# Forward transforms of two convolutions as three passes over high and low parts, with one transform table and kernel rows in natural order

## The chip, the core and the metric

The kernel runs on one core of a Trainium2 chip. The metric is the device time in microseconds (us) of one execution. The core has five engines that matter here: TensorE (PE, with its weight loads PEld), VectorE (DVE), ScalarE (ACT), GpSimd (POOL) and SyncE (SP). POOL and SP are used for issuing DMA transfers. Each engine runs its own list of instructions, whose order is fixed when the kernel is built; an instruction that waits for another engine holds up those behind it on its list.

## The reference

The reference is one transformer-like block on a sequence of L = 2048 tokens with D = 576 channels. All arrays are float32. A state-space convolution with a long kernel comes first, then a dense network of two layers:

```
P = exp((A * dt)[:, :, None] * pos)          # D x 128 x 2048 modes
K = 2 * einsum("dn,dnl->dl", C, P).real      # one kernel of length 2048 for each channel
y = irfft(rfft(u, 2L) * rfft(K, 2L))[:L] + u * D_skip

h = layernorm(x) * (1 + ca) + sa
x = x + ga * conv(h)
h = layernorm(x) * (1 + cb) + sb
x = x + gb * (relu(h @ w1) @ w2)             # 576 -> 4608 -> 576
```

The six vectors `sa, ca, ga, sb, cb, gb` come from silu(c) @ w_mod.

## The kernel before

The 2048 tokens are cut into four blocks of 512. For each block there is a convolution step, `conv(s)` for s = 0 to 3, and a feed-forward block of 36 steps, each of 128 hidden units. Counting through, steps 0 to 35 are block 0, 36 to 71 block 1, 72 to 107 block 2, and the rest block 3. The first 110 steps are done singly, and the rest, two at a time, in another form.

A single step g has two halves on PE. `first(g)` is 14 passes of 128x512 into the PSUM tile `hps` (L1368, two buffers). ACT turns it into `hh` (L1373, relu, the rounded high part), and DVE into `hl` (L1374, what the rounding left). `second(g)` is 14 passes into five accumulators `acc` (L1394): 9 or 10 of them use `hh`, the others `hl`. PE's order is `first(g)`, `second(g-1)`, `first(g+1)`, and so on. In the steps of block 0 DVE also makes the low parts of the weights (L1338, L1349, L1350), which later blocks load from DRAM.

While feed-forward block b runs, the next convolution, `conv(b+1)`, is produced in small pieces between its passes. `conv` is a Python generator whose `yield` values are estimated microseconds of DVE (or `None` for a piece on PE). The function `step(g)`, called four times in a step, takes pieces as long as the sum of estimates is below rate(b) times the number of calls. That sets when the pieces are written; the scheduler of the Tile framework then fixes the order on each engine.

A convolution of block s uses blocks of the FFT of the signal `U` and of the kernel `K`, in two halves of channels p = 0 and 1. It works like this:

- The kernel rows are loaded into a tile `kt` (one buffer, so the tile of p = 1 can only be loaded when the transforms of p = 0 have read it). `load_kt` does that with one DMA from POOL, L1291.
- `norm1` makes the normalised input `h` on DVE (L937, L938).
- `mm_K` and `mm_U` are the forward transforms: for each p, 8 fp32 matmuls of 128x288, each into one PSUM buffer (L854) that ACT empties into `Z` (L855). They use two tables of cosines and sines, `fcU` for the signal and `fcK` for the kernel. `fcK` has its rows in the order in which the kernel's rows stand in `kt`.
- Butterflies on DVE (L868 to L882) finish the transforms to `U_s_p` and `K_s_p`; L1001 and L1003 combine `K` with the block before it, `R`, which POOL loads from DRAM.
- `product` sums over earlier blocks: groups of DVE operations on 128x1152 (L1034, L1038, L1040). A product that isn't the first goes through a scratch tile `T` of half size, of which there are two buffers.
- The inverse: butterflies to `V_s_p`, 8 matmuls for each p (`ps_i`, L1061), and an addition to x (L1066).
- Statistics, transposes on PE (`ps_t`, L1155), and `xf`, `xh`, `xl`, `xs` (L1159 to L1168): these are what the feed-forward block of s works on.

The tiles of one size share a pool of seven buffers (`spec`), so a new one waits for an old one to be read.

Of the kernel before, what the change touches and what calls it, by code (L numbers as in the profile page):

```python
# [10 lines left out]
F32 = mybir.dt.float32  # L11
# [40 lines left out]
class KGen:  # L52
# [10 lines left out]
    def v(self, out, a, b, op):  # L63
        self.tc.keep_in_program_order(self.nc.vector.tensor_tensor(out, a, b, op=op))  # L64
# [511 lines left out]
class Body:  # L576
# [34 lines left out]
    def early(self, kg):  # L611

        nc, I, sm = self.nc, self.I, self.sm
        x2 = self.x2[0] = self.x2p[0].tile([P, 4, D], F32, tag="x2", bufs=1, name="x2_0")
        nc.sync.dma_start(out=x2, in_=I["x"][0:512, :].rearrange("(m n) d -> m n d", n=4))
        self.fcU, self.fcK, self.gc = (
            sm.tile([P, 4, 2, P], F32, name=n) for n in ("fcU", "fcK", "gc")
        )
        for t, n in ((self.fcK, "fck"), (self.fcU, "fcu"), (self.gc, "gc")):
            nc.sync.dma_start(out=t, in_=I[n])  # L620
        kept = self.tc.keep_in_program_order
        self.mv1 = mv = sm.tile([P, 4, 5], F32, name="mv1")
        for i in range(4):
            yield
            st = sm.tile([P, 2, 6], F32, tag="st", bufs=8, name="st0")
            for p in range(2):
                kept(nc.vector.bn_stats(out=st[:, p], in_=x2[:, i, p * PC : (p + 1) * PC]))
            kept(nc.vector.bn_aggr(out=mv[:, i, 0:2], in_=st))
        yield
        kept(nc.scalar.activation(mv[:, :, 2], mv[:, :, 1], AF.Sqrt, bias=self.eps))  # L630
        yield
        kept(nc.vector.reciprocal(mv[:, :, 3], mv[:, :, 2]))
        kept(nc.vector.scalar_tensor_tensor(
            mv[:, :, 4], mv[:, :, 0], -1.0, mv[:, :, 3], op0=ALU.mult, op1=ALU.mult
        ))
        self.h0 = h = kg.pw.tile([P, 4, D], F32, tag="W2", bufs=5, name="h_0")
        for i in (0, 2, 1, 3):
            kept(nc.scalar.activation(
                h[:, i], x2[:, i], AF.Identity, scale=mv[:, i, 3:4], bias=mv[:, i, 4:5]
            ))  # L640
        yield
        self.kt0 = kg.kt0
        kept(self.skip(self.kt0, 0, nc.vector))
        for i in (0, 2, 1, 3):
            kept(nc.vector.tensor_tensor(h[:, i], h[:, i], self.m["ca"], op=ALU.mult))
            kept(nc.vector.tensor_tensor(h[:, i], h[:, i], self.m["sa"], op=ALU.add))
        self.wm = {}
        for nm in ("sb", "cb"):
            self.wm[nm] = kg.pw.tile([P, 5, D], F32, tag="W2", bufs=5, name=f"wm_{nm}")
        yield  # L650
# [290 lines left out]
    def conv(self, s):  # L941
# [26 lines left out]
            h = self.spec(f"h_{s}").rearrange("p a b c -> p a (b c)")  # L968
        hv = h.rearrange("m n (dd p q) -> m n dd p q", dd=4, p=2)

        def mm_U(p, Z):
            return self.transform(lambda n2: hv[:, n2, :, p], self.fcU, Z, s == 0)

        def mm_K(p, Z):
            ktv = kt[p].rearrange("p (t dd g) q -> p t dd g q", t=2, g=2)
            if s == 0 and p == 1:
                self.skip(kt[p], p, Kept(self.tc, nc.gpsimd))
            src = lambda n2: ktv[:, n2 // 2, :, n2 % 2]
            if s == 0 and p == 1:
                return self.transform1(src, self.fcK, self.fcKn, Z)  # L980
            return self.transform(src, self.fcK, Z, s == 0)

        def spec_U(p, Z):
            U = self.spec(f"U_{s}_{p}")
# [92 lines left out]
        if s == 0:  # L1077
            yield from mm_K(0, ZK)
            yield from mm_U(0, ZU)
            Z1 = self.spec("Z")  # L1080
            yield from mm_U(1, Z1)
            for hook in ("first", "late", "rows"):
                yield hook
            kt[1] = kernel_tile(1)
            yield "weights"
            yield "mod"
            yield "mod"
            yield "mod"
            yield "high"
            yield from spec_U(0, ZU)  # L1090
            yield from spec_U(1, Z1)
            yield from spec_K(0, ZK)
            ZK = self.spec("Z")
            yield from mm_K(1, ZK)
            self.save(self.Rd[0][0], Ks[0], Kept(self.tc, nc.gpsimd))
        else:
            yield from both(self.norm1(x2, h), mm_K(0, ZK))
            kt[1] = kernel_tile(1)
            ZU = self.spec("Z")
            yield from both(spec_K(0, ZK), mm_U(0, ZU))  # L1100
            Z1 = self.spec("Z")
            yield from both(spec_U(0, ZU), mm_U(1, Z1))
            ZK = self.spec("Z")
            first[0] = self.load(self.Ud[0][0], "Ua")
            yield from both(spec_U(1, Z1), mm_K(1, ZK))
# [182 lines left out]

    def load_kt(self, kt, s, p, eng):
        kd = self.kd[s][p]  # L1290
        eng.dma_start(  # L1291
            out=kt,
            in_=bass.AP(tensor=kd.tensor, offset=kd.offset, ap=[[72, P], [9216, 16], [1, 72]]),
        )
# [409 lines left out]
            yield  # L1704

    def rate(self, b):
        return (2.15, 1.8, 1.4, 0.5)[b]


def after(n, g):  # L1710
# [79 lines left out]
```

## Time and profile before

| what | value |
|---|---|
| time, median of 3 runs | 1318.13 us (1313.81 to 1322.35) |
| the profiled execution: its own time | 1324.17 us |
| the profiled execution: span | 1322.4 us |
| mean granted clock of PE | 0.943 |
| PE busy | 1210.1 us, 92% |
| DVE busy | 993.3 us, 75% |
| ACT busy | 518.8 us, 39% |
| POOL busy | 161.1 us, 12% |

The span is the time from the first to the last instruction of the profiled execution. PE counts as busy while a matmul is in its pipeline, so 100% does not mean that passes follow each other at their shortest distance; the distance of two passes is read from the chain of waits or the timeline. In the chain, a row gives the start, the time and the number of instructions of one piece of the work that set the end. In the table of windows a row gives the busy time of each engine in a stretch of the span. Block 0 of the feed-forward network runs until about 553 us, block 1 until about 829, block 2 until about 1094.

### The profile page before, as it was taken

To read this page: it belongs to the slowest core of one execution; us is meant where nothing else is said; L and a number is where in the kernel's file an instruction comes from. 1 tells how busy PE (TensorE), PEld (TensorE's weight loads), DVE (VectorE), ACT (ScalarE), POOL (GpSimd) and SP (SyncE) were. 2 spreads that over 40 slices of the span, in tenths; PEclk is the share of its full clock that TensorE was granted. 3 is DMA by queue.
4 is the path that set the end of the run, shared out by engine and by line. 5 is a ranking of instruction groups with operands and counts; after the bars stand their busy time and mean duration, and the time that the engine had idled before them with its cause. 6 is when DMAs were issued, how large, how long until landed. Compare 5 with 4: busy or idle time off the path is not lost.

```text
span 1322.4 us, 27077 instructions
## 1 busy us (share of the span) xinstructions
PE 1210.1 (92%) x11094; PEld 973.6 (74%) x11094; DVE 993.3 (75%) x1538; ACT 518.8 (39%) x902; POOL 161.1 (12%) x256
## 2 busy tenths in 40 slices
PE   4665586899989998999999999999999999999998
PEld 3454464677767787787677887887888888998997
DVE  7899988999986999689468995467997237555543
ACT  5788423222223422622243225433222365434431
POOL 1676411011000100110001000100000000000000
PEclk9556787999989999999899999999999999999999
DMA  9758972988878967799779995877996658666641
GB/s 273 269 201 307 327 275 79 351 289 321 312 267 294 344 228 274 249 405 343 251 266 340 348 353 155 274 220 263 373 388 191 180 166 256 190 190 190 193 142 63
DMA packets 118032, 343.81 MB, mean 260 GB/s; under 512 B 17772, under 2 KB 21652, under 8 KB 107156
## 3 DMA queue, kind: packets, MB, share of 16 engines
q1 hardware_dynamic: 101332, 226.04, 51.0%
q0 software_dynamic: 16064, 114.67, 22.9%
q8 instruction: 87, 1.43, 0.4%
q10 hardware_dynamic: 512, 1.38, 0.3%
q14 instruction: 37, 0.30, 0.1%
HBM read 260.63 MB, written 81.40 MB: 259 GB/s over the span
## 4 chain that ended last, share of the span: by engine, by line
PE 71%; DVE 16%; DMA 7%; issue 3%; ACT 1%; POOL 1%; SPq 0%; ACTq 0%; DVEq 0%
PE acc L1394 28%; PE hps L1368 21%; PE hps L1495 7%; PE ps_f L854 5%; DMA L1d<-w 4%; PE kps L73 2%; PE kps L521 2%; PE ps_i L1061 2%; PE ph L73 2%; DVE T L486 1%; DVE W1r L488 1%; DMA x<-in_x_dram 1%; DVE Y L1040 1%; DVE T L64 1%; DVE w L1338 1%
## 5 line engine op out<-in xcount | busy, mean ns | idle before, releaser
L1394 PE MATMUL acc<-w,hh 128*128 128x512 f32 x1008 | 323.1, 403 | 3.2 <-ACT hh L1373 2.7
L1368 PE MATMUL hps<-xh,w 128*128 128x512 f32 x880 | 307.4, 410 | 0.7 <-ACT xh L49 0.7
L1394 PEld LDWEIGHTS acc<-w,hh 128*128 128x128 f32 x1008 | 187.4, 188 | 44.0 <-ACT hh L1373 3.6
L1368 PEld LDWEIGHTS hps<-xh,w 128*128 128x128 f32 x880 | 168.6, 192 | 38.7 <-ACT xh L49 1.3
L1394 PE MATMUL acc<-w,hl 128*128 128x512 f32 x504 | 195.1, 401 | 1.5 <-DVE hl L1374 1.5
L1343 ACT ACTIVATE w<-r 128x576 fp32r<-128x576 f32 x141 | 96.6, 685 | 229.7 <-PE acc L1394 195.2
L1368 PE MATMUL hps<-xl,w 128*128 128x512 f32 x440 | 175.7, 400 | 0.0
L1373 ACT ACTIVATE hh<-hps 128x512 fp32r<-128x512 f32 x110 | 65.7, 597 | 242.1 <-PE hps L1368 237.4
L1374 DVE SCALAR_TENSOR_TENSOR hl<-hps,hh 128x512 fp32r<-128x512 f32 x110 | 75.4, 685 | 113.1 <-ACT hh L1373 112.5
L1394 PEld LDWEIGHTS acc<-w,hl 128*128 128x128 f32 x504 | 94.3, 189 | 22.8 <-DVE hl L1374 3.0
L1333 ACT ACTIVATE w<-r 128x640 fp32r<-128x640 f32 x124 | 90.8, 732 | 42.7 <-DMA L1d<-w 42.1
L1368 PEld LDWEIGHTS hps<-xl,w 128*128 128x128 f32 x440 | 84.1, 191 | 18.3 <-DVE xl L49 0.4
L1040 DVE TENSOR_TENSOR Y<-Y,T 128x1152 f32<-128x1152 f32 x60 | 79.3, 1348 | 0.0
L73 PE MATMUL kps<-W,W 128*32 128x16 f32 x2304 | 39.4, 210 | 42.8 <-POOL W L70 28.4
L1368 PE MATMUL hps<-xs,w 128*128 128x512 f32 x220 | 78.0, 421 | 0.0
L855 ACT ACTIVATE Z<-ps_f 128x288 f32<-128x288 f32 x120 | 49.0, 410 | 71.6 <-PE ps_f L854 69.7
L73 PEld LDWEIGHTS kps<-W,W 128*32 128x32 f32 x2304 | 34.7, 142 | 56.4 <-POOL W L70 31.0
L521 PEld LDWEIGHTS kps<-W1r,W2r 128*32 128x32 f32 x3456 | 45.1, 113 | 38.8 <-issue 20.8
L521 PE MATMUL kps<-W1r,W2r 128*32 128x48 f32 (+2 forms) x3456 | 52.4, 202 | 15.9 <-ACT ker L531 9.3
L1503 DVE TENSOR_TENSOR C<-C,hps 128x256 f32<-128x256 f32 x17 | 7.1, 420 | 63.0 <-PE hps L1495 63.0
L1394 PE MATMUL acc<-hh,w 128*128 128x512 f32 x126 | 50.7, 402 | 0.0
L1394 PE MATMUL acc<-hl,w 128*128 128x512 f32 x126 | 49.9, 396 | 0.0
(307 smaller groups left out, 2197.9 us busy)
## 6 DMA issues: line engine op xcount, KB each, us to landing
r<-in_w_dram SPq DMA_DIRECT2D x144, 320.0 KB, 3.9
r<-in_w_dram SPq DMA_DIRECT2D x144, 288.0 KB, 4.9
w<-L2d SPq DMA_DIRECT2D x108, 288.0 KB, 4.1
w<-L1d SPq DMA_DIRECT2D x92, 320.0 KB, 3.9
W2r<-W2d POOLq DMA_DIRECT2D x18, 1536.0 KB, 8.5
W2d<-W SPq DMA_DIRECT2D x12, 1536.0 KB, 8.5
Ua<-Ud POOLq DMA_DIRECT2D x15, 1152.0 KB, 9.5
W<-W1d POOLq DMA_DIRECT2D x18, 768.0 KB, 9.4
```

The source lines that it names most:

```text
L73: self.tc.keep_in_program_order(self.nc.tensor.matmul(*args, **kw))
L521: nc.tensor.matmul(ps[32 * dd : 32 * dd + 32, q, :], W2[:, r, ch], W1[:, r, ch], start=(r == 0), stop=(r == 1),)
L854: nc.tensor.matmul(o, fc[:, n2, c, :], src(n2), start=True, stop=True)
L855: ev = nc.scalar.activation(Z[:, n2, c], ps[:, :PC], AF.Copy)
L1040: v(y, y, T, op=op or ALU.add)
L1333: copy(g - 1)(w1[g][:, 0], r1[g], AF.Copy)
L1343: copy(g)(w[:, 0:D], r2[g], AF.Copy)
L1368: nc.tensor.matmul(ps, a, x, start=(i == 0), stop=(i == 13))
L1373: nc.scalar.activation(hh, ps, AF.Relu)
L1374: nc.vector.scalar_tensor_tensor(hl, ps, 0.0, hh, op0=ALU.max, op1=ALU.subtract)
L1394: nc.tensor.matmul(acc[i], a, x, start=(f == 0 and seen[i] == 1), stop=(f == NF - 1 and seen[i] == (3 if i < 4 else 2)),)
L1495: nc.tensor.matmul(out, l, m, start=(i == 0), stop=(i == len(ops) - 1))
```

## The change

For the convolutions 2 and 3 (`s > 1`, the third and fourth) a forward transform is no longer an fp32 matmul. Its input is split in two parts: ACT rounds it to fp32r (the high part), DVE subtracts that from the input (the low part). `split` does it in two pieces of 128x576 for each call, into the two `half` buffers that the products' `T` also uses. The table is split in the same way, once, by `table`, before convolution 2; the parts go to the places of `fcK` and `fcU`. A transform is then three fp32r passes into the same PSUM tile: high by high, high by low, low by high.

Two further edits belong to it. The kernel rows of the convolutions 1 to 3 are loaded in natural order, so that one table serves `U` and `K`: eight DMAs, each into every eighth partition. The rates at which pieces of convolutions are taken are 1.86 and 1.46 instead of 1.8 and 1.4 in blocks 1 and 2.

```diff
@@ conv(s)
+        def split(x, name):
+            hi, lo = (
+                self.half(name + n).rearrange("p n (a b) -> p n a b", a=4).bitcast(F32R)
+                for n in "hl"
+            )
+            for i in range(2):
+                h, l = (t[:, 2 * i : 2 * i + 2] for t in (hi, lo))
+                nc.scalar.activation(h, x[i], AF.Copy)
+                v(l, x[i], h, op=ALU.subtract)
+                yield 0.8
+            return lambda n2: (hi[:, n2], lo[:, n2])
+
+        def table():
+            f = lambda t: t.rearrange("p n c k -> p (n c k)")
+            sm, shape = self.sm, [P, 4, 2, P]
+            hi = sm.tile(shape, F32R, tag="fcK", bufs=1, name="fch")
+            nc.scalar.activation(f(hi), f(self.fcU), AF.Copy)
+            t = self.spec("fct").rearrange("p a b c -> p (a b c)")[:, :1024]
+            v(t, f(self.fcU), f(hi), op=ALU.subtract)
+            yield 1.5
+            lo = sm.tile(shape, F32R, tag="fcU", bufs=1, name="fcl")
+            nc.scalar.activation(f(lo), t, AF.Copy)
+            self.parts = hi, lo
+
+        def thirds(p, Z, x, name):
+            hi, lo = self.parts
+            src = yield from split(x, name)
+            for n2 in (0, 2, 1, 3):
+                xh, xl = src(n2)
+                for c in range(2):
+                    ps = self.cps.tile([P, 512], F32, tag="cps", bufs=self.nps, name="ps_f")
+                    o = ps[:, :PC].rearrange("p (a b) -> p a b", a=4)
+                    fh, fl = hi[:, n2, c], lo[:, n2, c]
+                    for i, (a, b) in enumerate(((fh, xh), (fh, xl), (fl, xh))):
+                        nc.tensor.matmul(o, a, b, start=(i == 0), stop=(i == 2))
+                    nc.scalar.activation(Z[:, n2, c], ps[:, :PC], AF.Copy)
+                    yield None
+
         def mm_U(p, Z):
+            if s > 1:
+                return thirds(p, Z, [hv[:, 2 * i : 2 * i + 2, :, p] for i in range(2)], "hs")
             return self.transform(lambda n2: hv[:, n2, :, p], self.fcU, Z, s == 0)
...
+            if s > 1:
+                x = kt[p].rearrange("p (t dd g) q -> p t g dd q", t=2, g=2)
+                return thirds(p, Z, [x[:, i] for i in range(2)], "ks")
...
-            return self.transform(src, self.fcK, Z, s == 0)
+            return self.transform(src, self.fcU if s else self.fcK, Z, s == 0)
...
+            if s == 2:
+                yield from table()
@@ load_kt
+        if s:
+            for b in range(8):
+                eng.dma_start(
+                    out=kt[b::8],
+                    in_=bass.AP(
+                        tensor=kd.tensor, offset=kd.offset + 1152 * b,
+                        ap=[[72, 16], [9216, 16], [1, 72]],
+                    ),
+                )
+            return
@@ rate(b)
-        return (2.15, 1.8, 1.4, 0.5)[b]
+        return (2.15, 1.86, 1.46, 0.5)[b]
```

The line numbers of the changed kernel are later ones: `hl` is L1429, `acc` L1449, `hps` L1423, the products L1077, L1081 and L1083, the inverse L1104, the transposes L1200, the weights' low parts L1393, L1404 and L1405.

The change also moves work that it doesn't name. The first place is DVE in block 0, from the `hl` of step 21 on. Before, the normalisation of convolution 1 (`h_1`) and its first butterfly follow at once:

```order
L1374 SCALAR_TENSOR_TENSOR hl_5448<-hps_5429,hh_5447 128x512
L1338 TENSOR_TENSOR w1_5382<-r1_5269,w1_5382 128x640
L937 SCALAR_TENSOR_TENSOR h_1_5225<-x2_1_5203,mv_5309,m_ca_469 128x576
L937 SCALAR_TENSOR_TENSOR h_1_5225<-x2_1_5203,mv_5312,m_ca_469 128x576
L938 SCALAR_TENSOR_TENSOR h_1_5225<-h_1_5225,mv_5309,m_sa_551 128x576
L938 SCALAR_TENSOR_TENSOR h_1_5225<-h_1_5225,mv_5312,m_sa_551 128x576
L937 SCALAR_TENSOR_TENSOR h_1_5225<-x2_1_5203,mv_5315,m_ca_469 128x576
L937 SCALAR_TENSOR_TENSOR h_1_5225<-x2_1_5203,mv_5318,m_ca_469 128x576
L938 SCALAR_TENSOR_TENSOR h_1_5225<-h_1_5225,mv_5315,m_sa_551 128x576
L938 SCALAR_TENSOR_TENSOR h_1_5225<-h_1_5225,mv_5318,m_sa_551 128x576
L868 TENSOR_TENSOR W_5389<-Z_5226 128x576
L869 TENSOR_TENSOR W_5389<-Z_5226 128x576
```

In the changed kernel the same place, again from the `hl` of step 21 on, has only the weights' low parts (`w1`, `w2`) between one `hl` and the next:

```order
L1429 SCALAR_TENSOR_TENSOR hl_5462<-hps_5443,hh_5461 128x512
L1393 TENSOR_TENSOR w1_5389<-r1_5276,w1_5389 128x640
L1404 TENSOR_TENSOR w2_5543<-r2_5358,w2_5543 128x64
L1405 TENSOR_TENSOR w2_5543<-r2_5358,w2_5543 128x512
L1393 TENSOR_TENSOR w1_5471<-r1_5356,w1_5471 128x640
L1429 SCALAR_TENSOR_TENSOR hl_5540<-hps_5517,hh_5539 128x512
L1393 TENSOR_TENSOR w1_5549<-r1_5437,w1_5549 128x640
L1404 TENSOR_TENSOR w2_5612<-r2_5439,w2_5612 128x64
L1405 TENSOR_TENSOR w2_5612<-r2_5439,w2_5612 128x512
L1429 SCALAR_TENSOR_TENSOR hl_5609<-hps_5587,hh_5608 128x512
L1393 TENSOR_TENSOR w1_5618<-r1_5511,w1_5618 128x640
L1404 TENSOR_TENSOR w2_5692<-r2_5513,w2_5692 128x64
```

It goes on like that for steps 24 and 25; the normalisation now follows the `hl` of step 25, four steps later than before. On PE, the transforms of `kt` for convolution 1 stand ahead of the passes of step 26 instead of step 22, and those of its second half at steps 30 to 32 instead of step 25.

The second place is PE at the end of block 0. Before, the inverse of `V_1_1` (`ps_i`) stands among the passes of steps 33 and 34:

```order
L1394 MATMUL acc_0_3040<-hh,w_6161 128x512
L1061 MATMUL ps_i<-V_1_6117,gc 128x288 x2
L1394 MATMUL acc_0_3036<-w_6161,hh 128x512
L1394 MATMUL acc_0_3037<-w_6161,hh 128x512
L1394 MATMUL acc_0_3038<-w_6161,hh 128x512
L1394 MATMUL acc_0_3039<-w_6161,hh 128x512
L1368 MATMUL hps<-xs_2823,w_6106 128x512
L1368 MATMUL hps<-xh_2821,w_6106 128x512
L1061 MATMUL ps_i<-V_1_6117,gc 128x288 x2
```

In the changed kernel it stands behind the last passes of block 0 (step 35), and the transposes `ps_t` and the first passes of block 1 (`xs_6184`) behind it:

```order
L1449 MATMUL acc_0_3036<-w_6370,hl 128x512
L1449 MATMUL acc_0_3037<-w_6370,hl 128x512
L1449 MATMUL acc_0_3038<-w_6370,hl 128x512
L1449 MATMUL acc_0_3039<-w_6370,hl 128x512
L1104 MATMUL ps_i<-V_1_6131,gc 128x288 x8
L1200 MATMUL ps_t<-ident,h_6280 128x128 x2
L1200 MATMUL ps_t<-ident,h_6281 128x128 x2
L1200 MATMUL ps_t<-ident,h_6280 128x128 x2
L1200 MATMUL ps_t<-ident,h_6281 128x128 x2
L1423 MATMUL hps<-xs_6184,w_6278 128x512 x2
```

So no pass of block 0 is left on PE's list beside the end of convolution 1.

The third place is DVE in block 1, among the products of convolution 2. Before, no more than six products stand between two `hl`; this is one such stretch (`Y` is the sum over blocks, `T` the scratch tile):

```order
L1374 SCALAR_TENSOR_TENSOR hl<-hps,hh 128x512
L1066 TENSOR_TENSOR x_2_7739<-ps_i,x_2_7739 128x4x72
L1038 TENSOR_TENSOR T<-Ka,Ua 128x1152 x2
L1040 TENSOR_TENSOR Y_1_8640<-Y_1_8640,T 128x4x288 x2
L1038 TENSOR_TENSOR T<-Ka,Ua 128x1152
L1374 SCALAR_TENSOR_TENSOR hl<-hps,hh 128x512
L1040 TENSOR_TENSOR Y_1_8640<-Y_1_8640,T 128x4x288
```

In the changed kernel 22 products stand between the `hl` of steps 62 and 63; this is the first part of them, with the `hl` of step 62 ahead:

```order
L1429 SCALAR_TENSOR_TENSOR hl<-hps,hh 128x512
L1077 TENSOR_TENSOR Y_0_8416<-K_2_0_8057,Ua 128x4x288 x2
L1081 TENSOR_TENSOR T<-K_2_0_8057,Ua 128x1152 x2
L1083 TENSOR_TENSOR Y_0_8416<-Y_0_8416,T 128x4x288 x2
L1081 TENSOR_TENSOR T<-Ka,U_0_8123 128x1152 x2
```

Two `Y` and three more groups of two `T` and two `Y` follow before the `hl` of step 63. A second run, of 20 products, stands between the `hl` of steps 67 and 68, and those of steps 65, 66 and 67 stand directly behind each other. The last `K` transforms of convolution 2 stand behind pass 12 of `first(63)` on PE, and before at step 57; its last inverse stands in `first(70)`, and before in `first(68)`. The order of convolution 3 in block 2 is nearly the same in both kernels.

More of the change, by code (lines that the diff above doesn't have):

```diff
@@ L616, in early @@
         self.fcU, self.fcK, self.gc = (
-            sm.tile([P, 4, 2, P], F32, name=n) for n in ("fcU", "fcK", "gc")
+            sm.tile([P, 4, 2, P], F32, tag=n, bufs=1, name=n) for n in ("fcU", "fcK", "gc")
         )
```

## The prediction, made before the changed kernel was run

> **What bounds the kernel now.** I read the window table first, one stretch for each stage of the conveyor "feed-forward block of one token block beside the convolution of the next". Columns: window, length, then busy us and instruction count of PE, PEld, DVE, ACT and POOL, then granted clock, DMA share and GB/s.
>
> ```profile
> 420.00:528.00 108.00, 104.80 (x435) 79.77 (x433) 103.94 (x149) 36.89 (x70) 7.60 (x13) 0.98 0.75 270
> 528.00:553.00 25.00, 24.55 (x119) 19.08 (x118) 17.25 (x46) 17.85 (x34) 0.00 (x0) 1.00 0.72 230
> 652.00:670.00 18.00, 18.00 (x119) 14.39 (x118) 5.72 (x9) 4.85 (x8) 0.54 (x1) 0.90 0.81 274
> 723.00:760.00 37.00, 37.00 (x164) 30.56 (x163) 35.26 (x43) 11.12 (x18) 3.21 (x6) 1.00 0.98 354
> 760.00:831.00 71.00, 71.00 (x320) 57.51 (x318) 48.31 (x72) 29.64 (x51) 1.07 (x2) 1.00 0.73 250
> 925.00:1094.00 169.00, 169.00 (x753) 138.65 (x752) 114.28 (x153) 63.29 (x106) 4.24 (x8) 1.00 0.76 258
> ```
>
> Convolution 1 (420 to 528) is bound by DVE: 103.9 of 108 us busy. From 652 on PE is busy all the time, but in 723 to 760 (products of convolution 2) DVE has only 1.7 us to spare. Whatever PE saves after 652 is therefore gained only as long as DVE delivers each step's `hl` in time. The chain of waits then gives the unit prices on PE (columns: start, us, line, count):
>
> ```profile
> 723.17 3.17 PE hps L1368 x14
> 726.35 3.17 PE acc L1394 x14
> 670.37 0.48 PE ps_f L854 x2
> 676.73 0.56 PE ps_f L854 x2
> 1123.64 5.94 PE hps L1495 x50
> ```
>
> A pass of 128x512 takes 3.17/14 = 0.2265 us, so a step of 28 passes 6.35 us. One of the old fp32 transforms leaves two records and takes 0.48 to 0.56 us. A pass of 256 columns takes 5.94/50 = 0.119 us.
>
> **Part 1, the passes themselves.** 288 columns lie between the rows of 256 and 512: 0.119 x 288/256 = 0.134 or 0.2265 x 288/512 = 0.127 us, so three passes take 0.38 to 0.40. Against 0.53 (the middle of the two rows, weighted to 0.56) each of the 64 transforms of convolutions 2 and 3 saves 0.13 us: **-8 us** (bounds: 0.08 to 0.18, -5 to -11). Both lie where PE is the bound. The 16 copies on ACT and 16 subtractions on DVE, and `table`, are priced by their nearest relatives in the grouped instructions:
>
> ```profile
> L1343 ACT ACTIVATE w<-r 128x576 fp32r<-128x576 f32 x90 | 61.7, 686 | 139.6 <-PE acc L1394 136.7 <-DMA L2d<-w 2.6
> L1168 DVE TENSOR_TENSOR xl<-xf,xh 128x512 fp32r<-128x512 f32 x12 | 8.3, 688 | 7.4 <-ACT xh L1161 7.4
> ```
>
> Eight of each per convolution: 5.5 us on ACT, about 6 on DVE (8 x 0.7 to 0.78 for 576 columns). In block 2 (925 to 1094) DVE has 55 us to spare and ACT more: nothing. In block 1 they come ahead of the products and cost nothing by themselves; what they do there is hold buffers, next.
>
> **Part 2, the kernel rows and convolution 1.** One load becomes eight on POOL. The trace has one:
>
> ```profile
> 397.63 1.19 POOL L1291 DMA_DIRECT2D kt<-kd  x1 [22.32 <-DMA kd<-ker]
> DMA to landing us min/median/max: 5.4/8.6/14.7
> ```
>
> Eight issues cost POOL 1.2 us in all (if cost follows size) to 9.5 (if each costs the whole 1.19); POOL is nearly idle there. The dearer effect stands in the order: the K transforms of convolution 1, in front of step 22 before, now stand in front of step 26, and its `K_1` transforms at steps 30 to 32. Both engines keep to that order whether the rows land early or late. DVE's timeline of before gives the two ends (start, us, line):
>
> ```profile
> 419.32 0.69 DVE L1374 SCALAR_TENSOR_TENSOR hl<-hps,hh 128x512 fp32r<-128x512 f32 x1 [2.26 <-ACT hh L1373]
> 429.71 0.21 DVE L1349 TENSOR_TENSOR w<-r,w 128x64 fp32r<-128x64 f32 x1
> 429.84 0.68 DVE L1350 TENSOR_TENSOR w<-r,w 128x512 fp32r<-128x512 f32 x1
> 430.45 0.82 DVE L1338 TENSOR_TENSOR w<-r,w 128x640 fp32r<-128x640 f32 x1
> 527.97 0.68 DVE L1350 TENSOR_TENSOR w<-r,w 128x512 fp32r<-128x512 f32 x1
> ```
>
> From `hl` of step 21 (419.3) to the end of `V_1_1`'s butterfly (528.0) DVE takes 108.7 us, 104 of it busy. Now steps 22 to 25 hold only their `hl` and three weight subtractions, 0.6 + 1.6 = 2.2 us in 6.35, so DVE idles 4 x 4.15 = 16.6 us there. Steps 28 to 30 hold 11.5 us (one butterfly, three steps' own work) in 19.05: 7.5 idle. The three steps that no longer come after `V_1_1` add about 3.5 us of work ahead of it. So `V_1_1` is ready 16.6 + 7.5 + 3.5 = 27.6 us later, near 555.5. Before, PE filled the next stretch with the passes of steps 33 to 35 while inverse, statistics and transposes ran; now all passes of block 0 stand ahead of the inverse of `V_1_1`, and PE has nothing left. Before, the first pass of block 1 came at the start of this piece of the chain:
>
> ```profile
> 552.76 3.94 PE hps L1368 x17
> ```
>
> That is 24.8 us after `V_1_1`. With nothing beside it the tail may shrink to DVE's 17.25 busy us of that window. Block 1 then starts at 555.5 + 17.25 = 573 to 555.5 + 24.8 = 580 instead of 552.8: **+23 us** (middle; 19 to 27). If the idle of steps 28 to 30 falls away it is 12 to 20.
>
> **Part 3, convolution 2 beside block 1.** The order puts 22 products in a row between two `hl`, where before there were at most six. The price of a product on the chain:
>
> ```profile
> 509.52 2.63 DVE T L1038 x2
> 512.15 2.54 DVE Y L1040 x2
> L1374 DVE SCALAR_TENSOR_TENSOR hl<-hps,hh 128x512 fp32r<-128x512 f32 x91 | 62.5, 687 | 105.6 <-ACT hh L1373 105.0
> L1373 ACT ACTIVATE hh<-hps 128x512 fp32r<-128x512 f32 x91 | 54.3, 597 | 187.8 <-PE hps L1368 183.1 <-DVE x L1066 4.7
> ```
>
> 1.27 us for each product. First place, `hl` of step 63: two products go early; the others need the two `T` buffers, which now hold the parts of `kt_1` until the last `K_1` transform, after pass 12 of step 63. From there DVE needs 20 x 1.27 + 0.6 = 26.0 us to that `hl`. PE has 2 passes of `hps` 63, 14 of `acc` 62, 14 of `hps` 64 (there are two `hps` buffers) and 10 of `acc` 63 that need no `hl`: 40 x 0.2265 = 9.1. Stall: **+17**. Second place, `hl` of step 68: 20 products behind `hl` 67, which is ready 1.3 us after its passes (0.6 on ACT, 0.69 on DVE). 1.3 + 26.0, against 4 x 14 + 10 = 66 passes, 14.95 us: **+12**. Third, the end of the block:
>
> ```profile
> 805.52 1.09 PE ps_i L1061 x4
> 829.35 3.17 PE hps L1368 x14
> ```
>
> The last inverse ended at 806.6, and block 2 could begin 22.7 us later, covered by three and a half steps. The inverse of `V_2_1` now stands two steps later, with three half steps (9.5 us) left. A tail of 17.25 (window 528 to 553, as above) to 22.7 leaves 8 to 13; as the tail before may have had slack, I take **+6** (0 to 13).
>
> **Part 4, the clock.** After the wait for x at the start of convolution 2:
>
> ```profile
> 649.33 0.95 PE L521 MATMUL kps<-W1r,W2r 128*32 128x32 f32 x48 [2.69 <-ACT ker L531]
> 650.27 2.43 PE acc L1394 x5
> 653.58 4.31 PE hps L1368 x14
> ```
>
> 5 passes take 2.43 instead of 1.13 us and 14 take 4.31 instead of 3.17: 2.4 us lost after an idle time of 2.7. Three long idle times in block 0's end and block 1: 3 x 2.4 = **+7** (0 to 10). [...]
>
> **Sum.** -8 + 23 + 17 + 12 + 6 + 7 = +57 us. The profiled execution took 1324.17 us in all, so 1381 on its basis; it lies 6 us above the median of 1318.13, on whose basis it is **1375**. Its own range: low ends -11 + 19 + 13 + 8 + 0 + 0 = +29 (each stall 4 less, if a product costs 0.2 less), 1347; high ends -5 + 27 + 17 + 13 + 13 + 10 = +75, 1393.
>
> **Rivals.**
> *Not slower.* The passes are saved and nothing waits. Place: `hl` of step 63. It decides if PE has cover of 26 us or more there, 115 passes instead of 40, or DVE takes `hl` ahead of the queued products. For it: in 760 to 831 DVE was busy only 48 of 71 us. Against it: the two `hps` buffers, and that no row shows an instruction overtaken on DVE. 1318 - 8 = 1310, within 1%, chance 0.09. If in addition the products' competition with the steps of block 0 goes (420 to 528 has 3.2 us of idle PE, and its 12 steps with 48 transforms and inverses would need 12 x 6.35 + 48 x 0.53 = 101.6 of 108), about 6 more: 1304, faster, 0.08. [...]
>
> *Only one loss.* Either block 0 still finishes in time, because eight small loads and the later start cost less than four steps, or the bursts of block 1 drain faster. 1318 - 8 + 23 + 2 = 1335; or 1318 - 8 + 17 + 12 + 6 + 5 = 1350. For it: the order is a list, not a clock, and every wait there was worked out by hand. 0.18.
>
> *DMA takes over.* The eight loads of 256 rows of 288 bytes each land one behind the other at the 8.6 us of the single one, 7 x 8.6 = 60 us more per tile, 35 of them past the four steps that the order leaves. For it: the DMA share there is 0.75, and the loads of R, Ua and Ka queue behind them on POOL. 1375 + 35 = 1410, 0.05. Against it: total bytes are the same.
>
> The main case keeps 0.60. **Chances**: slower by over 1% (a difference of 1%, 13 us, is about what a measurement of this kernel can tell) 0.60 + 0.18 + 0.05 = 0.83; within 1% 0.09; faster 0.08. **Range**: from the lower end of the one-loss case (1335 less its 7 us of doubt, 1328) to just above the main case's high end, 1396; left out are the not slower cases and most of the DMA case.
>
> **What would show it.** Step 1: three records per transform at 0.13 us each; wrong if they take 0.17 or more. Step 2: DVE idle about 4 us in each of steps 22 to 25; PE idle for 15 to 25 us at the end of block 0, released by DVE or ACT at the transposes. Step 3: PE waits for `hl` twice in block 1, 17 and 12 us, behind runs of 20 products. Step 4: passes at 0.43 us after each of these. The prediction is wrong if PE stays over 98% busy in block 1, or if the first pass of block 1 comes before 560.

## The result, and the profile of the changed kernel

The changed kernel takes 1391.4 us (median of 6 runs, 1382.35 to 1395.6), and the kernel before 1318.05 us in the runs beside it. The ratio is 1.0534, with a 95% interval of 1.0486 to 1.0581. It is slower by about 73 us, where 57 were forecast. Its profiled execution has a span of 1380.5 us, 58 us above that of before, and a mean granted clock of 0.928.

The 73 and the 58 differ because of the time before the change begins to act. Up to `hl` of step 21 the lists of PE and DVE hold the same work in both kernels (ACT has one instruction more in the changed one, the rounding of the table, and POOL seven more issues of `kt`), but the profiled execution of the changed kernel reached that point at 407.6 us and that of before at 419.3. Others came there between these and 422, and one with another load of x (the kernel with one load) at 428. So I compare stages from that step on. Each entry is the time from one `hl` to another (starts on DVE's timeline), in us; the kernels below the second line are the experiments of the next section.

| profiled execution | step 21 to 37 (end of block 0) | 37 to 73 (block 1) | 73 to 109 (block 2) | 109 to the end |
|---|---|---|---|---|
| before | 138.1 | 283.1 | 258.0 | 223.9 |
| changed | 175.0 (+36.9) | 319.2 (+36.1) | 255.4 (-2.6) | 223.3 (-0.6) |
| eight loads alone | 175.2 (+37.1) | 318.5 (+35.4) | 258.1 (+0.1) | 223.4 (-0.5) |
| one load, tokens reordered | 139.1 (+1.0) | 298.7 (+15.6) | 277.1 (+19.1) | 229.8 (+5.9) |
| changed, old rates | 175.5 (+37.4) | 315.1 (+32.0) | 256.8 (-1.2) | 223.3 (-0.6) |
| before, tokens reordered | 138.1 (0.0) | 300.2 (+17.1) | 275.2 (+17.2) | 229.5 (+5.6) |
| change from convolution 2 on | 137.6 (-0.5) | 317.2 (+34.1) | 255.5 (-2.5) | 224.4 (+0.5) |
| the same, two queues | 137.8 (-0.3) | 289.7 (+6.6) | 256.4 (-1.6) | 222.7 (-1.2) |
| the same, old rates | 137.2 (-0.9) | 289.4 (+6.3) | 260.2 (+2.2) | 223.1 (-0.8) |
| the same, fp32 transforms | 138.1 (0.0) | 290.4 (+7.3) | 257.9 (-0.1) | 223.3 (-0.6) |
| change in convolution 3 only | 138.6 (+0.5) | 283.0 (-0.1) | 258.8 (+0.8) | 223.5 (-0.4) |
| the same, rate 1.55 | 137.8 (-0.3) | 283.3 (+0.2) | 256.3 (-1.7) | 224.0 (+0.1) |
| before, rate 1.55 | 137.5 (-0.6) | 283.9 (+0.8) | 258.0 (0.0) | 224.2 (+0.3) |
| convolution 3 only, rate 1.55, once more | 138.2 (+0.1) | 281.0 (-2.1) | 256.7 (-1.3) | 223.4 (-0.5) |

From step 21 on the change costs 36.9 + 36.1 - 2.6 - 0.6 = 69.8 us.

The windows of the changed kernel that answer to those of before (columns as there):

```profile
408.00:553.00 145.00, 125.98 (x500) 95.06 (x498) 110.50 (x158) 42.04 (x79) 10.86 (x20) 0.92 0.71 245
553.00:571.00 18.00, 10.80 (x23) 5.26 (x22) 8.25 (x29) 8.53 (x18) 0.00 (x0) 0.50 0.03 13
797.00:814.00 17.00, 0.53 (x3) 0.11 (x1) 17.00 (x15) 0.00 (x0) 1.69 (x3) 0.58 0.73 231
854.00:867.00 13.00, 0.92 (x5) 0.42 (x3) 13.00 (x12) 1.40 (x3) 0.00 (x0) 0.65 0.38 144
875.00:898.00 23.00, 22.99 (x114) 17.94 (x113) 13.46 (x35) 19.29 (x36) 3.90 (x7) 1.00 0.53 147
986.00:1153.00 167.00, 167.00 (x746) 136.91 (x744) 127.25 (x164) 63.56 (x107) 5.79 (x11) 1.00 0.77 264
```

In convolution 1 (408 to 553) DVE is busy 110.5 of 145 us where it was 103.9 of 108; it has 34.5 us of idle time, though it is the engine that sets the pace there. From 553 to 571, the end of convolution 1, PE is busy for 10.8 and DVE for 8.3 of 18 us, and PE's clock is 0.50. In 797 to 814 and 854 to 867 PE all but stands still while DVE is busy all the time. Who is waited for there is seen on PE's timeline (the bracket gives the idle time before the row, and the engine, result and line that ended it):

```profile
814.67 2.07 PE L1449 MATMUL acc<-w,hl 128*128 128x512 f32 x4 [17.14 <-DVE hl L1429]
835.59 1.20 PE L1449 MATMUL acc<-w,hl 128*128 128x512 f32 x4 [1.03 <-DVE hl L1429]
867.57 2.07 PE L1449 MATMUL acc<-w,hl 128*128 128x512 f32 x4 [12.65 <-DVE hl L1429]
```

These are the two stalls of 17 and 12 us that the order had shown. The chain of waits shows what lies in front of the first, from the last `K_1` transform on:

```profile
788.17 0.36 PE ps_f L1005 x2
...
788.55 2.63 DVE T L1081 x2
791.18 1.89 DVE Y L1083 x2
...
811.48 2.54 DVE Y L1083 x2
814.02 0.61 DVE hl L1429
...
814.67 2.50 PE acc L1449 x5
```

The first product that needs a `T` buffer starts when the last `K_1` transform has read its part, and 26 us later comes the `hl` that PE waits for. The five passes behind it take 2.50 us instead of 1.13.

The transforms themselves, in block 2, on the chain of the changed kernel and then of before:

```profile
906.30 0.39 PE ps_f L1005 x3
946.16 0.57 PE ps_f L1005 x3
```

```profile
866.33 0.48 PE ps_f L854 x2
900.87 0.56 PE ps_f L854 x2
```

Three passes take 0.39 to 0.40 us on PE in 23 of the 32 transforms of block 2, one fp32 matmul 0.48 to 0.49 in 23 of 32; the other nine of each take longer, as in the second rows. The means are 0.44 and 0.52. So the saving is 0.08 us for a transform, 2.5 us for the 32 of a convolution.

### The profile page after: what moved, and what is told of

It is laid out like the page before. It is cut to its first block, busy times and chain, and to the rows that moved or that the text cites. A ratio compares the mean times of both kernels' runs of the same rounds, so it can differ in the third digit from the quotient of the medians.

```text
span 1380.5 us, 27332 instructions
## 1 busy us (share of the span) xinstructions
PE 1214.6 (88%) x11158; PEld 972.5 (70%) x11158; DVE 1001.2 (73%) x1555; ACT 531.6 (39%) x920; POOL 180.6 (13%) x298
## 4 chain that ended last, share of the span: by engine, by line
PE 65%; DVE 19%; DMA 9%; issue 4%; ACT 2%; POOL 1%; SPq 1%; DVEq 0%; ACTq 0%; POOLq 0%
PE acc L1449 26%; PE hps L1423 19%; PE hps L1550 7%; DMA L1d<-w 3%; DVE T L1081 3%; PE ps_i L1104 3%; DVE Y L1083 2%; PE ps_f L1005 2%; PE ps_f L854 2%; DVE T L486 2%; PE kps L73 2%; DVE W1r L488 2%; PE ph L73 1%; PE kps L521 1%; DMA r<-in_w_dram 1%
## 5 line engine op out<-in xcount | busy, mean ns | idle before, releaser
L1449 PE MATMUL acc<-w,hh 128*128 128x512 f32 x1008 | 316.0, 396 | 0.6 <-ACT hh L1428 0.6
L1423 PE MATMUL hps<-xh,w 128*128 128x512 f32 x880 | 297.6, 397 | 1.2 <-ACT xh L49 1.2
L1449 PE MATMUL acc<-w,hl 128*128 128x512 f32 x504 | 196.7, 407 | 37.1 <-DVE hl L1429 37.1
L1449 PEld LDWEIGHTS acc<-w,hh 128*128 128x128 f32 x1008 | 186.7, 188 | 38.3 <-ACT hh L1428 1.0
L1423 PEld LDWEIGHTS hps<-xh,w 128*128 128x128 f32 x880 | 164.6, 189 | 35.9 <-ACT xh L49 2.5
L1429 DVE SCALAR_TENSOR_TENSOR hl<-hps,hh 128x512 fp32r<-128x512 f32 x110 | 75.3, 685 | 144.8 <-ACT hh L1428 144.8
L1423 PE MATMUL hps<-xl,w 128*128 128x512 f32 x440 | 176.6, 401 | 0.7 <-DVE xl L49 0.5
L1449 PEld LDWEIGHTS acc<-w,hl 128*128 128x128 f32 x504 | 95.9, 192 | 58.9 <-DVE hl L1429 39.8
L1423 PEld LDWEIGHTS hps<-xl,w 128*128 128x128 f32 x440 | 82.9, 188 | 19.0 <-DVE xl L49 1.7
L1083 DVE TENSOR_TENSOR Y<-Y,T 128x1152 f32<-128x1152 f32 x60 | 78.9, 1348 | 0.0
L1423 PE MATMUL hps<-xs,w 128*128 128x512 f32 x220 | 75.0, 414 | 1.8 <-DVE w L1393 1.0
L1104 PE MATMUL ps_i<-V,gc 128*128 128x288 f32 x136 | 50.1, 509 | 17.2 <-DVE x L1109 8.5
L1449 PE MATMUL acc<-hl,w 128*128 128x512 f32 x126 | 51.0, 405 | 6.1 <-DVE hl L1429 6.1
L1104 PEld LDWEIGHTS ps_i<-V,gc 128*128 128x128 f32 x136 | 31.0, 238 | 32.5 <-DVE x L1109 12.3
```

The source lines that it names most:

```text
L1083: v(y, y, T, op=op or ALU.add)
L1104: nc.tensor.matmul(ps[:, :PC], a, b, start=(i == 0), stop=(i == len(ops) - 1))
L1423: nc.tensor.matmul(ps, a, x, start=(i == 0), stop=(i == 13))
L1429: nc.vector.scalar_tensor_tensor(hl, ps, 0.0, hh, op0=ALU.max, op1=ALU.subtract)
L1449: nc.tensor.matmul(acc[i], a, x, start=(f == 0 and seen[i] == 1), stop=(f == NF - 1 and seen[i] == (3 if i < 4 else 2)),)
```

## The experiments

All ratios are against the kernel before on the same chip, with 95% intervals. Before, 1318 to 1324 us, is the median there.

### Is it the number of loads?

The first kernel is the kernel before with its loads of kernel rows cut in eight, nothing else:

```diff
-        eng.dma_start(
-            out=kt,
-            in_=bass.AP(tensor=kd.tensor, offset=kd.offset, ap=[[72, P], [9216, 16], [1, 72]]),
-        )
+        n = 16 if s else P
+        for b in range(0, P, n):
+            eng.dma_start(
+                out=kt[b : b + n],
+                in_=bass.AP(
+                    tensor=kd.tensor, offset=kd.offset + 72 * b, ap=[[72, n], [9216, 16], [1, 72]]
+                ),
+            )
```

> The kernel before with one edit: each load of kernel rows for the convolutions 1 to 3 is cut into eight loads of 16 neighbouring partitions (same rows to the same places; fp32 transforms, both tables and the old rates stay). Theory A (the eight loads alone move the order, as in the changed kernel): block 1 starts 25 us later than before, PE waits for hl twice in block 1, for 12 to 17 us each, behind runs of 20 or more products, and the saving of 8 us is missing: 1318 + 25 + 36 + 4 = about 1383, 1370 to 1395. Theory B (the eight loads cost block 0 alone, and the runs of products in block 1 come from the parts that hold the two T buffers): block 0 loses its 25 us, block 1 nothing: about 1343. Theory C (the number of loads does not matter, the passes and splits do): 1318.

Measured: 1395.63 us, ratio 1.0566 (1.0523 to 1.0609). The stage table has +37.1 and +35.4, the same as the whole change, and PE waits as there:

```profile
816.29 2.08 PE L1398 MATMUL acc<-w,hl 128*128 128x512 f32 x4 [13.35 <-DVE hl L1378]
869.48 2.07 PE L1398 MATMUL acc<-w,hl 128*128 128x512 f32 x4 [14.05 <-DVE hl L1378]
```

Theory A holds, though the time lies 0.6 us above its range, since block 0 lost 37 us and not 25. The whole loss comes from the eight loads, that of block 1 too. The parts in the `T` buffers only moved the first stall by 4 us, from 13.35 to 17.14; I had taken them for a cause of it. From step 21 on this kernel loses 37.1 + 35.4 + 0.1 - 0.5 = 72.1 us with fp32 transforms, and the changed one 69.8 with three passes; the 2.3 between them lie in block 2.

The third kernel is the changed one with the old rates, `(2.15, 1.8, 1.4, 0.5)`:

> The changed kernel with the old rates, 1.8 and 1.4. Theory A (the loads move the order): the order of block 0 and the two runs of products in block 1 stay, so the time does too: within 1% of the changed kernel, 1375 to 1400. Rival (the higher rates bunch the products): no stalls of more than 5 us in block 1, 1345 to 1355.

Measured: 1392.45 us, ratio 1.0529 (1.0482 to 1.0576), and the longest wait for `hl` is 17.1 us again. The rates are not the cause.

### The change with one load

The second kernel takes the eight loads out of the changed one. One table can then serve both transforms only if the tokens lie in the same order as the kernel rows, so the rows of x are loaded and stored in that order:

```diff
-        if s:
-            for b in range(8):
...
+def rows(t, b, i=None):
+    step = 4 * D if i is None else D
+    return bass.AP(
+        tensor=t.tensor, offset=t.offset + b * 512 * D + (i or 0) * D,
+        ap=[[4 * D, 8], [32 * D, 16], [1, step]],
+    )
...
-    r["fcu"] = dft(j)
-    r["fck"] = dft(8 * (j % 16) + j // 16)
+    r["fcu"] = r["fck"] = dft(8 * (j % 16) + j // 16)
-    m = np.arange(P)[None, None, :]
+    m = (8 * (j % 16) + j // 16)[None, None, :]
```

> The changed kernel with one load again for each tile of kernel rows, in the old order of partitions. So that one table still serves both, the 128 rows of x (four tokens each) are loaded and stored in that same order of partitions, and the table of the inverse has its columns in that order. Three passes, splits and new rates stay. Theory A: block 0 goes as in the kernel before (its order is the same word for word up to names), no run of more than eight products in block 1, the saving of 8 us shows: about 1310, 1303 to 1318. Theory B (the splits hold the T buffers and cost the stalls of block 1): no loss in block 0, 20 to 36 us in block 1: 1335 to 1350. Theory C (the splits cost DVE and ACT more than PE saves): 1320 to 1335.

Measured: 1366.9 us, ratio 1.0317 (1.0266 to 1.0368). No theory gave that. Block 0 went as before (+1.0), and no wait of PE for `hl` is longer than 4.5 us, but blocks 1 and 2 lost 15.6 and 19.1 us. The chain of waits and PE's timeline of this kernel show where; the first row has its counterpart in the kernel before in the third:

```profile
648.42 22.76 DMA x<-in_x_dram
899.13 0.61 PE L1004 MATMUL ps_f<-ksh,fch 128*128 128x288 f32 x1 [18.57 <-ACT Z L1005]
```

```profile
630.40 14.06 DMA x<-in_x_dram
```

The load of x for convolution 2 took 22.8 us instead of 14.1, and the one for convolution 3 ended so late that PE waited 18.6 us at its first transforms. This was my edit, not the change under study. Its control is the kernel before with the reordered tokens alone, three passes and all else left out:

> The kernel before with the tokens' order of the one-load experiment alone: rows of x loaded and stored in the partition order of the kernel rows, tables to match; fp32 transforms, one load for each tile of kernel rows, old rates. The instructions stand on each engine as in the kernel before. That experiment was 43 us slower than before, with 10.7 us of it at step 48 and 16.7 at step 75, where the load of x took 22.8 and 18.8 us. Theory A (the loads and stores of permuted rows take longer, and that is all of it): about as slow as the one-load experiment, 1355 to 1370. Theory B (the splits and three passes make the loss): within 1% of before.

Measured: 1369.38 us, ratio 1.0367 (1.0322 to 1.0412); +17.1 and +17.2 us in blocks 1 and 2. Theory A: the reordered tokens cost all of it. The change without its eight loads has 1.0317 where its control has 1.0367, with intervals of 0.5% on each, and from step 21 on its profiled execution lost 41.6 us where the control lost 39.9. The two measures point in opposite ways, so the pair shows no loss from the three passes and splits, and no gain either.

### Block 0 and block 1 apart, and the same loads in another place

Here convolution 1 keeps its one load and its own table, and the change begins with convolution 2:

```diff
-            return self.transform(src, self.fcU if s else self.fcK, Z, s == 0)
+            return self.transform(src, self.fcK, Z, s == 0)
...
-        if s:
+        if s > 1:
             for b in range(8):
```

> The changed kernel, but convolution 1 keeps its single load of kernel rows and its own table; eight loads, one table and three passes only for the convolutions 2 and 3. The order of block 0 is then that of before, that of block 1 as in the changed kernel. Theory A (the two blocks lose independently): block 0 within 3 us of before, block 1 +36 us, block 2 -3: 1318 + 33 = 1351, 1343 to 1358. Rival (the late end of block 0 carries on into block 1 as stalls): block 1 loses less than 20 us, under 1338.

Measured: 1352.88 us, ratio 1.0258 (1.0198 to 1.0318). Block 0 lost nothing (-0.5), block 1 +34.1, block 2 -2.5: theory A, and each block's loss is its own. The stalls are the same to the hundredth:

```profile
783.35 2.07 PE L1449 MATMUL acc<-w,hl 128*128 128x512 f32 x4 [17.14 <-DVE hl L1429]
836.49 2.07 PE L1449 MATMUL acc<-w,hl 128*128 128x512 f32 x4 [12.65 <-DVE hl L1429]
```

The next kernel issues every second one of these loads from another queue:

```diff
-                eng.dma_start(
+                (self.nc.sync if b % 2 else eng).dma_start(
                     out=kt[b::8],
```

> As the experiment with eight loads for the convolutions 2 and 3 only, but of each eight loads four are issued by SP and four by POOL. The number, size and pattern of the loads stay. In the order the K transforms of convolution 2 then stand at step 53 instead of 56 (before: 52), and no run of more than eight products stands between two hl. Theory A (the place in the order makes the loss, not the loads on the chip): block 1 loses less than 8 us, block 2 gains 3: 1313 to 1323. Rival (eight small loads are slow on the chip, wherever they stand): block 1 +25 us or more, 1340 and above.

Measured: 1327.66 us, ratio 1.0050 (1.0027 to 1.0074). The same 16 loads, as small and as scattered, now cost 6.6 us in block 1 instead of 34.1, and no wait for `hl` is longer than 0.9 us (the table of PE's waits; columns: total, times, longest):

```profile
PE ps_f L1005 <- ACT Z L1006: 3.8, 7, 0.8
PE acc L1449 <- DVE hl L1429: 1.7, 3, 0.9
```

Theory A: the place in the order makes the loss, though the time is 5 us above the range given for it. DVE's timelines agree: 22 products in a row and then 20 (19 with the old rates) stand between two `hl` of block 1 in the changed kernel, with eight loads alone, with the old rates, and with the change from convolution 2 on, the four kernels that lose 32 to 36 us there; in all others the longest such run is nine. What is left has another place: the `K` transforms still stand a step later than before, the next eight stand in a row, and with one PSUM buffer PE waits for ACT at seven of them. Of the two waits above, 5.5 us in all, the kernel before has none. With the old rates on top:

> As the experiment with two queues, with the old rates 1.8 and 1.4. The end of convolution 2 stands half a step to a step later. Theory A (rates move pieces by less than the cover): within 5 us of the experiment with two queues. Rival (the rates were needed because of the added DVE pieces): 8 us or more slower, at the end of block 1.

Measured: 1331.23 us, ratio 1.0081 (1.0054 to 1.0108): within 4 us of the kernel with the new rates, so theory A. Block 1 has the same +6.3, and block 2 is 3.8 us longer than with the new rates, 3.1 of them in one wait of PE (more on it below). And with fp32 transforms instead of three passes, loads and rates alike:

> The experiment with two queues, but with fp32 transforms: eight loads and the one table for the convolutions 2 and 3, rates 1.86 and 1.46, no splits. It tells what the three passes are worth in a kernel whose loads are the same. Theory (0.09 us a transform, 2.9 us a convolution, less waits of PE for its one PSUM buffer where eight transforms stand in a row): block 1 within 3 us of the 289.7 us of the experiment with two queues, block 2 258 to 260. Rival (the splits themselves made the 6.6 us that block 1 lost there): block 1 at 283 to 285.

Measured: 1329.38 us, ratio 1.0088 (1.0067 to 1.0109). Block 1 lies 0.7 us above its sister with three passes and block 2 1.5 us above. So without the splits block 1 loses as much. But it loses it elsewhere, in two waits for `hl` and none at the transforms:

```profile
PE acc L1404 <- DVE hl L1384: 5.5, 2, 3.2
```

What the splits cost in block 1 is therefore not shown by this pair. The three passes are worth about 2 us of the stages. By the ratios, 1.0088 against 1.0050, it may be 5, but the intervals touch.

### Convolution 3 alone

Last, the change where the order did not suffer: one table, eight loads and three passes for convolution 3 only.

```diff
-            if s > 1:
+            if s > 2:
...
-            if s == 2:
+            if s == 3:
                 yield from table()
...
-        return (2.15, 1.86, 1.46, 0.5)[b]
+        return (2.15, 1.8, 1.46, 0.5)[b]
```

> One table, eight loads and three passes for convolution 3 alone (table split ahead of it); everything for the convolutions 1 and 2 as before, rates 1.8 and 1.46. Block 2 gained 1.2 to 2.6 us in the kernels with three passes there, and its order hardly moves. Theory (the passes save 0.09 us a transform, 32 x 0.09 = 3 us, and nothing is lost elsewhere): block 0 and 1 within 1 us of before, block 2 -2 to -3, 1315 to 1319, a ratio of 0.997 to 1.000. Rival (eight loads for convolution 3 lose something there that the changed kernel hid behind its late start): block 2 slower than before.

Measured: 1323.48 us, ratio 1.0047 (1.0022 to 1.0073). Blocks 0 and 1 are as before, but block 2 is 0.8 us longer, not 2 to 3 shorter. The stages hold 0.9 us of the 6 that the ratio gives; where the rest arose they do not show. With a rate of 1.55 in block 2:

> As the kernel with three passes in convolution 3 alone, with a rate of 1.55 in block 2: the end of convolution 3 stands two steps earlier. If the time from step 109 on (a wait for a weight and the first pairs) depends on that end, 1 to 3 us less than with 1.46; if not, the same within 1 us.

Measured: 1317.95 us, ratio 1.0004 (0.9988 to 1.0020). Block 2 is now 1.7 us shorter than before, while the time from step 109 on is unchanged, so that does not hang on the end of convolution 3. PE's timelines show what does differ in block 2: one wait, at the seventh `K` transform of convolution 3 in the kernel with rate 1.46 (first row) and at the eighth in this one:

```profile
857.71 0.40 PE L1005 MATMUL ps_f<-ksh,fch 128*128 128x288 f32 x1 [3.26 <-ACT Z L1006]
855.47 0.40 PE L1005 MATMUL ps_f<-ksh,fch 128*128 128x288 f32 x1 [1.03 <-ACT Z L1006]
```

The chain of waits leads from both back to the load of x for convolution 3. Without that wait block 2 takes 258.8 - 3.3 = 255.5 and 256.3 - 1.0 = 255.3 us. The changed kernel, whose PE has no wait in block 2, takes 255.4, and the fp32 kernels with one or eight loads 257.9 to 258.1. So the three passes do save about 2.5 us in convolution 3, and a wait at its start can take the saving back. The kernel with two queues and old rates waits 3.1 us at the same transform. The control of that rate, and the same kernel once more beside it:

> The kernel before with one number changed: rate 1.55 instead of 1.4 in block 2. It is the control for the kernel with three passes in convolution 3 and that rate, which came out at 1.0004 of before. If the three passes are worth 3 us in convolution 3, this one comes out at 1.002 to 1.003 (about 1321); if they are worth nothing there, at 1.000; if the rate itself is what helps, below 1.000 and faster than that kernel.

> The same kernel as the one with three passes in convolution 3 alone and rate 1.55, beside its control on one chip. Same question: 3 us less than the control if the passes save 0.09 us each and nothing is lost, the same time if the saving is lost again.

Measured: 1321.35 us, ratio 1.0015 (0.9994 to 1.0035), for the kernel before with rate 1.55, and 1318.51 us, ratio 0.9993 (0.9971 to 1.0015), with the three passes beside it. The difference of 3 us is about what 32 x 0.08 gives, but it lies inside the intervals, and the control's own interval holds both the 1.000 and the 1.002 of its two cases. No kernel that was run beats the kernel before by more than its interval.

## Why the prediction was right, and where its terms were off

The direction, the two places and their mechanism came out as forecast, and 1391.4 lies in the range of 1328 to 1396, near its upper end. The sum was 16 us short of the medians and 13 short of the 69.8 us of the stages: 11.5 in block 0 (36.9 where 23 and a third of the clock's 7 were forecast), 1.4 in block 2, and nothing in block 1 (36.1 against 17 + 12 + 6 + 5 - 4 = 36). That block 1 fits so well is partly luck: the 6 did not come, and smaller waits that I had not counted (two of 1 us for `hl`, one for `ker`) took part of its place, and the passes saved less than 4. By its own steps:

- **The passes (-8).** Most took 0.39 to 0.40 us, within the 0.38 to 0.40 forecast. But I set 0.53 for the old ones, near their mean (0.52 in block 2), against the shortest of the new ones, whose mean is 0.44: longer rows come with both. The saving is 0.08 us each, 2.5 us in block 2; if it is as much in block 1, which no pair of runs isolates, some 5 in both.
- **Eight loads on POOL.** They cost 0.56 us each, 4.5 in all, between the bounds of 1.2 and 9.5. That the rows land early and the engines keep to the order anyway is shown by the three rows below (POOL's timeline with the last four of the eight, the landing times of all loads of `kt`, and the chain of waits): the last issue ended at 391.7, no load took longer than 13.6 us to land, and the rows were first used at 434.6.

```profile
389.51 2.21 POOL L1338 DMA_DIRECT2D kt<-kd  x4
DMA to landing us min/median/max: 3.3/5.9/13.6
434.59 0.48 PE ps_f L854 x2
```

- **Convolution 1 (+23, measured +37).** Two steps failed: what comes ahead of `V_1_1`, and the tail after it. `V_1_1` was ready 145.7 us after `hl` of step 21 instead of 108.7, so 37 us later and not 27.6. By the windows DVE idled 34.5 us where it had idled 4.1, 30 more (24 forecast), and was busy 6.6 us more (3.5 forecast; at the 2.2 us that the prediction gives a step, three steps make 6.6). Steps 22 to 25 are right: DVE idles in them 15.5 us by its timeline, where 16.6 were forecast. In steps 28 to 30 it idles 13.9, nearly twice the 7.5 of the forecast, and 1.8 more in step 31. I had given each of these steps 6.35 us of passes, but the late `U` transforms stand among their passes as well, and step 28 took 11.7 us. The timeline shows DVE waiting there:

```profile
465.99 0.69 DVE L1429 SCALAR_TENSOR_TENSOR hl<-hps,hh 128x512 fp32r<-128x512 f32 x1 [5.19 <-ACT hh L1428]
472.32 0.69 DVE L1429 SCALAR_TENSOR_TENSOR hl<-hps,hh 128x512 fp32r<-128x512 f32 x1 [2.26 <-ACT hh L1428]
```

 The tail, for which 17.25 to 24.8 us were forecast, did not shrink. The 24.8 of before was a misreading: the row at 552.76 holds the last three passes of the first step of block 1 and the 14 of the second. The first pass of block 1 came at 544.8, right behind its input `xs`, so 16.9 us after `V_1_1` (528.0). In the changed kernel it came 17.4 us after (553.3 to 570.7):

```profile
544.83 0.62 PE L1368 MATMUL hps<-xs,w 128*128 128x512 f32 x2
570.72 2.07 PE L1423 MATMUL hps<-xs,w 128*128 128x512 f32 x4 [0.82 <-DVE xs L1209]
```

 And the first `hl` of block 1 came 27.5 us after `V_1_1` (580.8) against 27.1 before (555.1 - 528.0). With nothing beside it the tail could have been shorter, but its work on PE ran at a clock of 0.50 until 574.5 (1.00 in 574.5 to 581). The chain of waits has four matmuls of the inverse at 2.30 us there, four times over, where they took 0.97 in the kernel before:

```profile
530.37 0.97 PE ps_i L1061 x4
554.22 2.30 PE ps_i L1104 x4
```

 That slow tail also kept the idle time of PE, put at 15 to 25 us at this place, down to 7.2 in 553 to 571.
- **The two stalls of block 1 (+17 and +12).** Measured 17.14 and 12.65. The working by hand (products at 1.27 us, against the passes that need no `hl`) held. The cause that I gave for the first one was only a part: with no part in a `T` buffer it is 13.35 (eight loads alone), so the run of products in the order is enough for a stall.
- **The end of block 1 (+6).** It did not come. PE is busy 22.99 of 23 us from 875 to 898.
- **The clock (+7).** Of the 36.1 us of block 1, 32.0 are four waits for `hl` (17.14, 12.65, and two near 1 us) and 1.0 a longer wait for `ker` than before. That leaves 3.1 for the slow passes less what the three passes saved; the two are not told apart. Behind the two stalls PE was busy 5.50 and 3.80 us at a granted clock of 0.50, at half pace (two passes 0.43 us apart, at 816.54 and 816.97 and again at 869.44 and 869.87, where 0.23 is the distance at 792.61 and 792.84), so they cost some 4.7 us on top. The row quoted above has 5 passes in 2.50 us; with the two passes and the four of an inverse that follow, the first stall cost about 3 us on top, near the 2.4 forecast. The clock was 0.50 for 5.6 us behind the first stall (814.7 to 820.3) and for 3.9 behind the second (867.6 to 871.5), and 1.00 in the windows that follow (820.25 to 826 and 871.45 to 875):

```profile
814.67:820.25 5.58, 5.50 (x12) 3.76 (x13) 5.43 (x10) 0.68 (x1) 0.00 (x0) 0.50 0.69 248
867.57:871.45 3.88, 3.80 (x8) 2.62 (x9) 3.88 (x7) 0.68 (x1) 0.00 (x0) 0.50 0.11 14
```

- **The rivals.** "Not slower" fell with the stalls. "Only one loss", at 1335 to 1350, is nearly what happens when the change starts with convolution 2 (1352.9). "DMA takes over" is excluded by the landing times (13.6 us at most, where it needed 60 more) and by the kernel with two queues. That the eight loads alone carry the change's whole loss in block 1 too was not among my cases: I had counted it to the splits.

What stays open is why the order moves when the loads are cut: only what the scheduler wrote was seen, not its reason. Buffers of their own for the parts were not tried.

## What to carry to other kernels

Where a scheduler writes each engine's list, an edit is worth what its list is worth: here 64 transforms, each 0.08 us shorter, were paid for with 70 us, because the work behind a load cut in eight stood four steps later in the order, while the data lay ready and unused. Before a change is timed, count what stands between two results that the busiest engine waits for, and set it against the work that does not need them; that sum gave both stalls to within 0.7 us. And give each step the time of everything that stands in it, not of its usual work.

## What the runs showed of the hardware

- Reordered rows made the same load slower: with the rows of x in groups of 8 times 16 rather than 128 in a line (9216 bytes each in both), it took 22.4 us instead of 14.1 at convolution 2 (first row, the reordered tokens alone). At convolution 3 the kernel with one load took 18.8 (third row) where the kernel before took 7.0 (second):

```profile
638.39 22.42 DMA x<-in_x_dram
x<-in_x_dram POOLq DMA_DIRECT2D x1, 1152.0 KB, 7.0
x<-in_x_dram POOLq DMA_DIRECT2D x1, 1152.0 KB, 18.8
```

 Why the reordered load takes longer, no run here shows.
- One issue from POOL cost 1.17 us for the whole load of `kt` (128 partitions with 16 runs of 288 bytes each) and 0.56 for an eighth of it: an eighth of the size cost half, so cutting in eight cost nearly four times as much POOL time (8 x 0.56 = 4.5 us). The load of x, also 128 partitions but one run of 9216 bytes each, cost 0.53, so here the number of partitions alone did not make an issue dear. The issues of `kt` and x in the kernel before, and of `kt` in the changed one (min/median/max in ns, then the time of the first and the last):

```profile
L1291 POOL DMA_DIRECT2D kt<-kd x6: 1173/1173/1185, 397.6 to 855.5; - x6
L49 POOL DMA_DIRECT2D x<-in_x_dram x3: 530/531/542, 374.8 to 846.2; - x3
```

```profile
L1338 POOL DMA_DIRECT2D kt<-kd x48: 558/558/594, 387.3 to 902.2; - x48
```

- The time before step 21 differed by up to 14 us between executions with the same lists on PE and DVE and the same load of x (407.6 for the changed kernel, 422 with the old rates), which is a fifth of the effect studied; the stage table, which starts behind it, repeats within about 2 us where nothing was changed.
